# Loading the output weights in the 33rd round of scores instead of ahead of the first queries' fetches

## The chip, the cores and the metric

The kernel runs on one core of one Trainium2 chip. The metric is the time of one execution on the device, in microseconds (us). Beside it stands the span of a profiled execution, from its first to its last instruction.

## The reference

Two independent operators are computed in float32, and their outputs are put side by side. A is a long convolution whose kernel comes out of a state-space model with 576 channels and 128 states; B is attention with 32 query heads of 18 elements over 2048 positions, which all share one key and one value head.

```python
def _A_ref(u, A_re, A_im, B_re, B_im, C_re, C_im, log_dt, Dskip):
    dt = jnp.exp(log_dt)[:, None]
    logdA = dt * (A_re + 1j * A_im)
    P = jnp.exp(logdA[:, :, None] * l[None, None, :])          # l = 0..2047
    K = jnp.einsum("dn,dnl,dn->dl", Cc, P, dt * Bc).real
    ...                                                         # causal convolution of u with K
    return y + u * Dskip[None, None, :]

def _B_ref(x, wq, wk, wv, wo):
    q = (x @ wq).reshape(B, S, H, Dh).transpose(0, 2, 1, 3)     # H = 32, Dh = 18
    k, v = x @ wk, x @ wv
    p = softmax(einsum("bhqd,bkd->bhqk", q, k) * Dh ** -0.5)
    o = einsum("bhqk,bkd->bhqd", p, v)
    return o.transpose(0, 2, 1, 3).reshape(B, S, H * Dh) @ wo

return jnp.concatenate([_A_ref(...), _B_ref(...)], axis=-1)
```

The change concerns `wo`, the matrix of the last product of B.

## The kernel before, in words

**Attention.** The 2048 queries are worked in four chunks `c` of 512. In a chunk, heads are taken in pairs: a pair has its queries in one tile `aug` (two heads at partitions 0 and 64, 55 rows each: the query as a high part, again, a low part, and a row with a bound on the scores). For every block `kb` of 128 keys and every pair, `scores` (L454) makes a 128 x 1024 tile of scores with two matmuls (L461), `exponentials` (L465) turns it into P on ACT (L469), and `product` (L753) multiplies P by the values on PE (L760). A group is four heads, so two pairs; its 16 key blocks make 32 score tiles. When a group is done, its sums are copied out of PSUM (`gather`, L472, a DVE copy into `o`) and stored in DRAM (`od`). After eight groups, a chunk is normalized and multiplied by `wo` (`normalize`, `outproj`; the matmuls are at L174, in the helper `matmul4`).

**Rounds.** The main loop runs over 1024 score tiles in rounds of three (`for r in range(0, len(pairs), NS)`, L772, NS = 3), for three buffers of scores. A round issues its scores, then the products that are due and the exponentials, then fills the time left with other work (`fill`), then calls `fetch`. Round 33 is the one with r = 96; there the fourth group begins.

**Queries.** `qproj` (L325) computes the queries of some seven heads at a time. They go to DRAM (`qd`) by DMA, from POOL (L404), save those of the very first heads, which go from SP. `fetch` (L444) loads them as `aug` tiles from SP (L450) for the pairs up to five ahead, as far as they have been computed; the ring has five tiles, so a fetch also waits until PE is done with the scores of the pair that had its tile.

**The convolution** (`class Conv`) is cut into twelve pieces. Each makes tables on DVE (`tab`, L1100 and on, by the recorder at L104), kernel samples on PE (`kg`, L1124), transforms on PE (L174, with the matrix `dft`), products on DVE, and transforms back. Its transfers go by SP too.

**The order.** The order of PE, ACT and DVE is written out when the program is built: a planner with estimated costs (`Clock`, `Stream`, `fill`) decides which piece of side work goes in between the rounds. SP's loads and stores stand in the order in which the program issues them, all in one queue. `load_wo` (L320) writes five zeros with a DVE MEMSET that isn't part of the planner's estimates, then issues five loads of `wo` from SP; each waits for the MEMSET:

```python
def load_wo(self):
    self.nc.vector.memset(self.wo[0:1, :, 0:1], 0.0)
    for m, (m0, mn) in enumerate(MT):
        self.nc.sync.dma_start(self.wo[:mn, m, :], self.a["wo"][m0:m0 + mn, :])
```

In the kernel before, it is called at the head of `main` (L703). At that place the SP queue has just been given the key rows (`kaug`), the query weights, the transform matrix `dft` and the inputs `u` and `dsk` of the first two pieces of the convolution (`Conv.start`, L1277). What comes behind it is the first call of `fetch`, at the end of the first round.

Of the kernel before, what the change touches and what calls it, by code (L numbers as in the profile page):

```python
# [176 lines left out]
class Attention:  # L177
# [521 lines left out]
    def main(self, conv, flag):  # L699
        nc, K = self.nc, self.k  # L700
        conv.beside = lambda: self.o_left + self.q_left
        side = self.side_work
        self.load_wo()  # L703
        K.t = K.v = K.a = self.o_free = 0.0
        K.fill = 0.0
        side.ready = 0.0
        for st in conv.streams:
            st.ready = 0.0
        prep = Stream(self.prepare(), K, 99.0)
        pairs = [(c, g, kb, j) for c in range(NCH) for g in range(8) for kb in range(16) for j in range(2)]  # L710
        state = dict(credit=0.0, filled=0.0)

        def holder():
            return next((st for st in [side] + conv.streams if st.holds), None)

        def force(done):
            while not done():
                st = holder()
                (side if st is None else st).advance()
                self.fetch(self.group)  # L720

        def fill(then):

            t, idle = K.t, 0.0
            more = True
            while more:
                more = False
                credit = state["credit"] - (K.t - t - idle)
                urgent = self.due < self.step + 8
                late = self.late()  # L730
                for st in (prep, side, conv) if urgent else (prep, conv, side):

                    if st is side and side.kind == "p" and not (urgent or side.holds) and conv.lags(self.step):
                        continue
                    spare = credit - 0.3 if st is not side or urgent or late or side.holds else 0.0
                    wait = then - K.t - (1.2 if st is side and not urgent and not side.holds and self.units > 0.6 * self.step + HEAD else 0.15)
                    if st.go(self.step, max(spare, wait, 0.3 * (st is side and side.holds and conv.lags(self.step) and credit > -1.0)), holder()):
                        more = True
                        break
                else:  # L740

                    at = min((x for x in (st.event() for st in [prep, side] + conv.streams) if x > K.t), default=then)
                    if at < then - 0.5:
                        idle += at - K.t
                        K.t = at
                        more = True
            t += idle
            if K.t > t:
                K.t += 0.03
            state["filled"] += K.t - t  # L750
            state["credit"] = max(state["credit"] - (K.t - t), -0.8)

        def product(n):  # L753
            nonlocal o_ps
            c, g, kb, _ = pairs[2 * n]
            if kb == 0:
                fill(self.o_free)
                o_ps = self.ps_o.tile([P, CT], F32, tag="o", name=f"ops{c}_{g}")
            for j in range(4):
                nc.tensor.matmul(o_ps[32 * j:32 * j + 32, :], self.v[:, kb, :], pts[2 * n + j // 2][:, j % 2, :],  # L760
                                 start=(kb == 0), stop=(kb == 15), tile_position=(0, 32 * j))
            K.pe(0.88, done[2 * n + 1] + 0.1, self.o_free if kb == 0 else 0.0)
            read[n] = K.t + 0.2
            state["credit"] -= 0.88
            if kb == 15 and (c, g) != (NCH - 1, 7):
                self.gather(c, g, o_ps)
                if g == 7:
                    self.todo.append((c, range(5)))
                if c == NCH - 1 and g in LATE:
                    self.todo.append((c, LATE[g]))  # L770
        o_ps, pts, done, read, behind = None, {}, {}, {}, 0
        for r in range(0, len(pairs), NS):  # L772
            new = range(r, min(r + NS, len(pairs)))
            self.step = new[-1] // 2
            ss = {}
            for i in new:
                c, g, kb, j = pairs[i]
                if (g, kb, j) == (0, 0, 0):
                    self.od[c] = self.dr.tile([8 * P, CT], F32, tag="od", name=f"od{c}")
                force(lambda: 16 * c + 2 * g + j in self.ready)  # L780
                ss[i] = self.scores(i, c, 2 * g + j, kb, 0.335 if i == r else 0.215)
            K.t += 0.22
            for i in new:

                while (i - NP) // 2 >= behind:
                    product(behind)
                    behind += 1
                c, g, kb, j = pairs[i]
                pts[i] = self.exponentials(i, c, 2 * g + j, kb, *ss[i], read.get((i - NP) // 2, 0.0))
                done[i] = K.a  # L790
            s = self.step

            state["credit"] = min(state["credit"] + NS / 2 * (0.88 + min(max((TOTAL - state["filled"]) / max(LAST - s, 20), 0.45), 0.7 if s < 384 else 0.9)), 1.2 + 0.88)

            def free():

                return max(K.s[(r + NS + j) % NS] - 0.22 * j for j in range(NS))
            while behind < r // 2:
                fill(free() - 0.88 * (r // 2 - behind))

                if behind == r // 2 - 1 and K.t + 0.88 > free() + DEFER:
                    break
                product(behind)
                behind += 1
            fill(free())
            c, g, kb, j = pairs[new[-1]]
            self.group = (new[-1] + 1) // 32
            self.fetch(self.group)
            nxt = 16 * c + 2 * g + 3
            if kb >= 12 and nxt < 64:  # L810
                force(lambda: nxt in self.ready)
        while behind < len(pairs) // 2:
            product(behind)
            behind += 1

        while self.todo or self.busy or holder() or any(m == 0 for _, _, m in self.rest):
            if self.todo or self.busy:
                prep.advance()
            elif holder() or self.outs:
                (holder() or side).advance()  # L820
        conv.drain()
        nc.vector.tensor_scalar(flag, self.ubound[0:1, :], LIMIT / (2 * SCALE), None, op0=ALU.is_le)
        self.finish(NCH - 1, self.part, o_ps, self.w4, self.b4)
# [596 lines left out]
```

## Time and profile before

| | |
|---|---|
| runs shown | 1220.51, 1227.37, 1228.71 us; median 1227.37 |
| the profiled execution's own time | 1227.15 us |
| its span | 1224.8 us |
| mean granted PE clock | 0.985 of full speed |
| PE busy | 1146.8 us (94%) |
| ACT busy | 1032.8 us (84%) |
| DVE busy | 983.7 us (80%) |
| moved by DMA | 102.13 MB |

PE is TensorE (matmuls; PEld are its weight loads), ACT ScalarE, DVE VectorE, POOL GpSimd, SP SyncE; a q behind the name (SPq) means the engine's queue, which issues DMAs. A row of a timeline gives the start in us, the duration in us, engine, line, operation and tiles (out<-in), shape and count; the bracket at its end is the time the engine was idle just before, and what ended it ("issue": nothing that the profile shows). A row of waits gives the total in us, the number of times and the longest. A row of stretches gives the stretch, its length, the busy time of PE, PEld, DVE, ACT and POOL with their counts, then the granted PE clock, the busy share of the DMA engines and the GB/s moved. Rows of DMA queues give packets, MB and the share of 16 engines.

### The profile page before, as it was taken

To read this page: it belongs to the slowest core of one execution; us is meant where nothing else is said; L and a number is where in the kernel's file an instruction comes from. 1 tells how busy PE (TensorE), PEld (TensorE's weight loads), DVE (VectorE), ACT (ScalarE), POOL (GpSimd) and SP (SyncE) were. 2 spreads that over 40 slices of the span, in tenths; PEclk is the share of its full clock that TensorE was granted. 3 is DMA by queue.
4 is the path that set the end of the run, shared out by engine and by line. 5 is a ranking of instruction groups with operands and counts; after the bars stand their busy time and mean duration, and the time that the engine had idled before them with its cause. 6 is when DMAs were issued, how large, how long until landed. Compare 5 with 4: busy or idle time off the path is not lost.

```text
span 1224.8 us, 32944 instructions
## 1 busy us (share of the span) xinstructions
PE 1146.8 (94%) x13852; PEld 469.6 (38%) x13852; DVE 983.7 (80%) x1608; ACT 1032.8 (84%) x1091; POOL 119.2 (10%) x210
## 2 busy tenths in 40 slices
PE   5989899999899999899999989999989999899997
PEld 1434333444243434334344324444333444334333
DVE  4758988987988976895897996897998896796653
ACT  2778889889889888988888988888889888998993
POOL 2230310120310000011020000001150000000000
PEclk9999899999899999999999999999989999999999
DMA  7542323123343112213224011313142313012111
GB/s 225 149 139 81 127 79 101 51 64 96 107 131 107 35 38 93 81 39 113 82 90 145 28 71 54 102 52 105 37 123 88 106 36 90 21 51 82 35 40 42
DMA packets 61712, 102.13 MB, mean 83 GB/s; under 512 B 17692, under 2 KB 28570, under 8 KB 61048
## 3 DMA queue, kind: packets, MB, share of 16 engines
q1 hardware_dynamic: 47046, 85.32, 21.7%
q0 software_dynamic: 13824, 14.07, 4.5%
q8 instruction: 110, 1.80, 0.6%
q10 hardware_dynamic: 690, 0.60, 0.2%
q14 instruction: 42, 0.34, 0.1%
HBM read 55.66 MB, written 42.89 MB: 80 GB/s over the span
## 4 chain that ended last, share of the span: by engine, by line
PE 64%; DVE 21%; ACT 6%; DMA 4%; issue 4%; POOL 0%; SPq 0%; DVEq 0%; ACTq 0%
PE ops L760 26%; PE s L461 19%; ACT P L469 6%; PE op L174 5%; DVE tab L104 3%; PE q L339 3%; DVE acc L104 3%; DVE ks L104 3%; PE kg L1124 3%; PE iy L174 3%; DVE pt L104 2%; DMA xr<-xT 2%; PE hu L174 1%; PE hk L174 1%; DVE o L108 1%
## 5 line engine op out<-in xcount | busy, mean ns | idle before, releaser
L469 ACT ACTIVATE P<-s 128x1024 f32<-128x1024 f32 x1024 | 967.9, 1030 | 156.4 <-PE s L461 154.3
L760 PE MATMUL ops<-P,v_sb 128*32 128x512 f32 x4096 | 520.3, 604 | 8.2 <-DVE o L108 8.0
L461 PE MATMUL s<-aug,kaug 55*128 55x512 f32 x2048 | 362.1, 441 | 23.7 <-ACT P L469 19.0
L461 PEld LDWEIGHTS s<-aug,kaug 55*128 55x128 f32 x2048 | 168.9, 185 | 328.9 <-ACT P L469 281.4
L760 PEld LDWEIGHTS ops<-P,v_sb 128*32 128x32 f32 x4096 | 115.3, 110 | 161.2 <-issue 123.1
L404 POOL DMA_DIRECT2D qd<-qh x116 | 67.2, 585 | 536.0 <-DVE qh L108 535.9
L174 PE MATMUL op<-wo_sb,oT 126*32 126x288 f32 (+1 forms) x1112 | 83.1, 423 | 7.3 <-DVE ob L108 5.5
L339 PE MATMUL q<-x,wq_sb 128*32 128x256 f32 x1360 | 87.5, 391 | 1.0 <-DVE un L116 1.0
L108 DVE COPY ksb<-kg 128x192 f32<-128x192 f32 x48 | 17.4, 362 | 62.9 <-PE kg L1124 61.7
L104 DVE TENSOR_TENSOR tab<-tab 128x576 f32<-128x576 f32 (+1 forms) x72 | 59.1, 821 | 1.5
L104 DVE TENSOR_TENSOR tab<-tab,tt 128x576 f32<-128x576 f32 (+1 forms) x72 | 59.1, 820 | 1.5
L339 PEld LDWEIGHTS q<-x,wq_sb 128*32 128x32 f32 x1360 | 41.2, 112 | 47.9 <-issue 22.3
L104 DVE TENSOR_TENSOR tt<-f,sum 128x576 f32<-128x576 f32 (+1 forms) x72 | 58.8, 816 | 0.0
L104 DVE TENSOR_TENSOR tab<-sum,r 128x576 f32<-128x576 f32 (+1 forms) x72 | 58.7, 816 | 0.0
L104 DVE TENSOR_TENSOR tab<-r,dif 128x576 f32<-128x576 f32 (+1 forms) x72 | 58.7, 815 | 0.0
L174 PEld LDWEIGHTS op<-wo_sb,oT 126*32 126x32 f32 (+1 forms) x1112 | 32.9, 112 | 53.5 <-issue 21.8
L104 DVE TENSOR_TENSOR acc<-acc,pt 128x1728 f32<-128x1728 f32 (+2 forms) x36 | 48.7, 1353 | 0.5
L104 DVE TENSOR_TENSOR pt<-us,ks 128x1728 f32<-128x1728 f32 (+2 forms) x36 | 48.6, 1350 | 0.2
L1124 PEld LDWEIGHTS kg<-tab 128*32 128x32 f32 x2304 | 36.0, 110 | 24.5 <-issue 10.8
L1124 PE MATMUL kg<-tab 128*32 128x64 f32 x2304 | 41.7, 220 | 2.1 <-DVE tab L104 1.3
L104 DVE TENSOR_TENSOR ks<-ks 128x576 f32<-128x576 f32 (+1 forms) x48 | 40.9, 852 | 0.7
L104 DVE TENSOR_TENSOR u<-u,iy 128x384 f32<-128x384 f32 x24 | 13.3, 554 | 31.7 <-PE iy L174 31.4
(134 smaller groups left out, 967.1 us busy)
## 6 DMA issues: line engine op xcount, KB each, us to landing
aug<-qd SPq DMA_DIRECT2D x124, 110.0 KB
od<-o SPq DMA_DIRECT2D x31, 256.0 KB
fr<-stage SPq DMA_DIRECT2D x10, 624.0 KB
qd<-qh POOLq DMA_DIRECT2D x24, 216.0 KB, 4.3
u<-u SPq DMA_DIRECT2D x12, 384.0 KB
kd<-ksb SPq DMA_DIRECT2D x12, 384.0 KB
kt<-kd SPq DMA_DIRECT2D x48, 96.0 KB
outa<-u SPq DMA_DIRECT2D x12, 384.0 KB
```

The source lines that it names most:

```text
L104: return self.v.tensor_tensor(out, *a, **k)
L108: return self.v.tensor_copy(out, *a, **k)
L174: nc.tensor.matmul(ps[j:e], w[:, j:e], x, start=start, stop=stop, tile_position=(0, j))
L339: nc.tensor.matmul(ps[o, 256 * f:256 * f + 256], w[:, k, i], xt[:, k, x], start=(k == 0), stop=(k == 4), tile_position=(0, 32 * j))
L404: q.dma_start(qd[h:h + n, row + d:row + d + nd, cs], src[i1:i1 + n * nd, :cs.stop - cs.start].bitcast(F32))
L461: nc.tensor.matmul(ps[:, j, :], self.kaug[r, kb * P:(kb + 1) * P], t[r, :], start=True, stop=True)
L469: nc.scalar.activation(pt, ps, AF.Exp, scale=SCALE)
L760: nc.tensor.matmul(o_ps[32 * j:32 * j + 32, :], self.v[:, kb, :], pts[2 * n + j // 2][:, j % 2, :], start=(kb == 0), stop=(kb == 15), tile ...
L1124: nc.tensor.matmul(ps[32 * g:32 * g + 32, d, :], t[:, :32], t[:, 32:], start=(j == 0), stop=(j == 1), tile_position=(0, 32 * g))
```

## The change

The call of `load_wo` is taken out of the head of `main` and put into round 33, behind that round's scores, products and exponentials and ahead of its fill. `load_wo` itself, its MEMSET and its five loads are the same. Nothing else changes, and the planner's estimates are the same with and without it.

```diff
--- before.py
+++ after.py
@@ -700,7 +700,6 @@
         nc, K = self.nc, self.k
         conv.beside = lambda: self.o_left + self.q_left
         side = self.side_work
-        self.load_wo()
         K.t = K.v = K.a = self.o_free = 0.0
         K.fill = 0.0
         side.ready = 0.0
@@ -789,6 +788,9 @@
                 pts[i] = self.exponentials(i, c, 2 * g + j, kb, *ss[i], read.get((i - NP) // 2, 0.0))
                 done[i] = K.a
             s = self.step
+            if r == 96:
+
+                self.load_wo()
 
             state["credit"] = min(state["credit"] + NS / 2 * (0.88 + min(max((TOTAL - state["filled"]) / max(LAST - s, 20), 0.45), 0.7 if s < 384 else 0.9)), 1.2 + 0.88)
```

## The prediction

> **What bounds the kernel now.** I read the page first, for what the whole span is made of; then the waits of PE in time order, because PE carries the chain; then the order of the SP queue around the five loads that move; then the same at the place they move to.
>
> ```profile
> span 1224.8 us, 32944 instructions
> PE 1146.8 (94%) x13852; PEld 469.6 (38%) x13852; DVE 983.7 (80%) x1608; ACT 1032.8 (84%) x1091; POOL 119.2 (10%) x210
> PE 64%; DVE 21%; ACT 6%; DMA 4%; issue 4%; POOL 0%; SPq 0%; DVEq 0%; ACTq 0%
> q8 instruction: 110, 1.80, 0.6%
> ```
>
> PE is busy for 94% of the span and carries 64% of the chain that ended last; transfers carry only 4% of it. A moved load is therefore worth something only where PE stands still because of it. The order of instructions on PE, ACT and DVE is written out by the planner and does not change, so what PE loses in one place it does not make up by doing something else first. The last row is needed below: 110 transfers of instructions of 16 KB each, beside 2 x 13852 PE instructions, make one such transfer for about 252 PE instructions. That is PE's own code, which arrives while it runs.
>
> The only long stop of PE near the moved loads is in the first 80 us. The timeline of PE and of ACT there:
>
> ```profile
> 58.59 1.90 PE L760 MATMUL ops<-P,v_sb 128*32 128x512 f32 x16
> 66.29 0.28 PE L174 MATMUL up<-sel_sb,aw 128*32 128x8 f32 x16
> 68.92 0.73 PE L461 MATMUL s<-aug,kaug 55*128 55x512 f32 x4 [2.35 <-issue]
> 70.01 0.46 PE L461 MATMUL s<-aug,kaug 55*128 55x512 f32 x1 [0.35 <-DMA aug<-qd]
> 70.65 0.61 PE L461 MATMUL s<-aug,kaug 55*128 55x512 f32 x1 [0.18 <-DMA aug<-qd]
> 71.19 3.44 PE L760 MATMUL ops<-P,v_sb 128*32 128x512 f32 x16
> 74.56 0.96 PE L461 MATMUL s<-aug,kaug 55*128 55x512 f32 x6
> ...
> 64.44 2.86 ACT L469 ACTIVATE P<-s 128x1024 f32<-128x1024 f32 x3 [0.19 <-PE s L461]
> 69.55 2.86 ACT L469 ACTIVATE P<-s 128x1024 f32<-128x1024 f32 x3 [2.25 <-PE s L461]
> 75.19 5.61 ACT L469 ACTIVATE P<-s 128x1024 f32<-128x1024 f32 x6 [2.78 <-PE s L461]
> ```
>
> Three things are to be seen. At 66.57 PE stops for 2.35 us with nothing named that it waits for. Then the two score matmuls of the next pair of heads wait 0.35 and 0.18 us for their queries (aug). Then sixteen products take 3.44 us where sixteen of the same took 1.90 us at 58.59. ACT pays for all of it: 2.25 and 2.78 us idle, against 0.19 in the round before.
>
> ```profile
> 58.00:62.00 4.00, 4.00 (x80) 1.85 (x82) 2.26 (x4) 3.30 (x4) 2.17 (x4) 1.00 0.96 228
> 62.00:66.00 4.00, 4.00 (x94) 1.71 (x82) 0.69 (x3) 3.81 (x5) 2.36 (x5) 1.00 0.99 289
> 66.00:70.00 4.00, 1.31 (x28) 0.64 (x21) 3.90 (x12) 1.75 (x3) 0.50 (x1) 1.00 0.86 295
> 70.00:74.00 4.00, 3.82 (x18) 0.94 (x18) 3.55 (x5) 2.40 (x3) 0.61 (x1) 0.61 0.64 226
> ...
> q1 hardware_dynamic: 1133, 2.27, 90.8%
> q0 software_dynamic: 148, 0.12, 5.0%
> q14 instruction: 2, 0.02, 0.4%
> ...
> q8 instruction: 1, 0.02, 4.0%
> ```
>
> The first four rows are four stretches (last three columns: granted clock, busy share of the DMA engines, GB/s). The transfers are saturated from 58 to 70 (0.96, 0.99, 0.86) and the clock is 0.61 right after the stop. The rows behind the first "..." are the queues of the nine microseconds from 57 to 66: no instruction transfer of q8 at all. The last is from 66 to 68: there it is. In the eight microseconds from 58 to 66 PE issued 80 + 82 + 94 + 82 = 338 instructions, more than the 252 of one transfer. So I read the unnamed 2.35 us as PE having run out of code, its next block standing behind other transfers.
>
> What stood there, from the timeline of the SP queue, its waits from 52 to 75, and the sizes:
>
> ```profile
> 54.66 0.60 SPq L964 DMA_DIRECT2D u<-u  x1
> 55.86 4.39 SPq L323 DMA_DIRECT2D wo_sb<-wo  x5
> 61.13 9.84 SPq L450 DMA_DIRECT2D aug<-qd  x10
> ...
> SPq L450 <- DMA wo_sb<-wo: 4.1, 4, 2.0
> SPq L450 <- DMA u<-u: 1.6, 1, 1.6
> ...
> wo_sb<-wo SPq DMA_DIRECT2D x4, 283.5 KB
> wo_sb<-wo SPq DMA_DIRECT2D x1, 162.0 KB
> ```
>
> The five wo loads are issued from 55.86 to 60.25, the first query fetches only from 61.13, and these wait another 4.1 us in all for wo loads to land before SP may issue on. The wo loads are 4 x 283.5 + 162 = 1296 KB, 1.33 MB, which at the 289 GB/s of 62 to 66 is 4.6 us of all the transfer capacity there is.
>
> **The change part by part.**
>
> (1) The five loads leave the front of the queue. The queries that PE used at 70.01 and 70.65 lay behind 4.6 us of wo; without it they are there by about 65.4 to 66.0, and the round that needs them could begin its third score at about 67.3 (the exponential that frees the last score buffer ends at 64.44 + 2.86). The 0.53 us of named waiting goes, with over a microsecond to spare. The code block appears after 66.0; to cost nothing it must come 2.35 us earlier, and 4.6 us of transfers ahead of it are gone. So that wait goes too, by about the same spare. Without the stop the slow products, 3.44 against 1.90, lose their cause: 1.54 us. By PE: 2.35 + 0.35 + 0.18 + 1.54 = 4.42. By ACT: 2.25 + 2.78 less two ordinary gaps of 0.19 = 4.65. I take 4.5. Bounds: at most the whole idle time of ACT, 5.03; at least the named waits alone, 0.53, if the code comes no earlier. Below nothing is excluded here, since nothing is put in the place that is left.
>
> The Trainium skill (page "Runtime: NRT & Kernel Launch", section "Instruction fetch mechanics") speaks against my reading: it has code come in blocks of 256 instructions, the next while the present one runs, and calls the cost mostly hidden. The block size agrees with the 252 of the page row; "hidden" does not agree with an unnamed stop of 2.35 us that ends after the missing block came. By that rule the stop has another cause and stays, and the sum would be 0.53 us.
>
> (2) Does DVE let the gain through? It must have been idle here, since PE's products feed it:
>
> ```profile
> 79.69 0.69 DVE L108 COPY o<-ops 128x512 f32<-128x512 f32 x1 [6.07 <-PE ops L760]
> ```
>
> It stood 6.07 us waiting for this very product. A shift of 4.5 to 5.0 fits into that with 1 us left, and what DVE does next starts from this copy. If that cover were gone, the gain would be cut to what DVE has idle. So the later work on all engines moves forward as one block.
>
> (3) The loads arrive in the 33rd round. The order of SP there, what DVE does, and the stretches:
>
> ```profile
> 153.69 1.59 SPq L450 DMA_DIRECT2D aug<-qd  x4
> 162.09 0.34 SPq L478 DMA_DIRECT2D od<-o  x1
> ...
> 158.57 0.69 DVE L108 CAST qh<-q 128x512 fp32r<-128x512 f32 x1 [1.27 <-PE q L339]
> ...
> 152.00:156.00 4.00, 4.00 (x50) 1.50 (x42) 3.83 (x8) 3.67 (x5) 0.00 (x0) 1.00 0.30 103
> 156.00:160.00 4.00, 4.00 (x40) 1.64 (x36) 2.69 (x4) 3.35 (x5) 0.45 (x1) 1.00 0.16 49
> 160.00:164.00 4.00, 3.13 (x26) 0.80 (x22) 3.96 (x10) 3.03 (x4) 4.00 (x8) 1.00 0.48 128
> ...
> L321 DVE MEMSET wo_sb<- x1: 62/62/62, 31.7 to 31.7; 1x5 f32 x1
> L174 PE MATMUL op<-wo_sb,oT x1112: 402/406/690, 411.6 to 1203.8; 126*32 126x288 f32 x154, 72*32 72x288 f32 x32
> ```
>
> The four fetches at 153.69 end the 32nd round's work, so the loads stand behind them, wait for their MEMSET (62 ns) in DVE's order, and stand ahead of the store of o at 162.09. SP has nothing to issue from 155.28 to 162.09, 6.8 us; five issues took 4.39 us with their waits at the old place. So SP is late for nobody. The MEMSET goes ahead of a 1.27 us idle of DVE: nothing, and 0.06 us if that idle were gone. The 1.33 MB fall on DMA engines busy 0.16 to 0.48; they are through in some 5 to 7 us. Nobody waits for them before 411.6. What is behind them on SP (the store of o, later loads for the convolution) and on POOL (the queries of later heads, of which the first are used many rounds on) is not in demand there. PE's code: 50 + 42 + 40 + 36 + 26 + 22 = 216 instructions in 12 us, so one block lasts about 14 us here against 6 us at the front; a block that comes 5 us late is still in time. I put this part at nothing, bounded below by nothing and above by the price of the third rival.
>
> **Sum.** The profiled execution took 1227.15 us, 2.35 around its span of 1224.8. 1227.15 - 4.5 + 0.0 = 1222.65, which I give as 1222.6. The three runs shown have the median 1227.37, so this execution stands for them; but they spread from 1220.51 to 1228.71.
>
> **Rivals.** *First: the code comes no earlier.* u, the fetches themselves and POOL's stores of queries still fill the engines from 58 to 66, and the block may stand behind all of these just as well. Against it: 1.33 MB of what passed before it is gone. Gain 0.53, time 1226.6. The same time comes out of the skill's rule above. Chance 0.17.
>
> *Second: the gain is taken back.* PE reaches a later wait sooner and stands there longer, because DVE is at its own pace. For it: DVE is 21% of the chain. Against it: its 6.07 us of idle and its start from PE's product. With all taken back 1227.1; chance 0.10.
>
> *Third, the other side: the wo loads starve PE's code at the new place.* If the next block is asked for just as the loads begin and PE has less than about 5 us of instructions left, PE stops for the whole 4.6 us of the burst, some 1.3 us for the block (4.0% of 16 engines over the two microseconds from 66 to 68), and 1.54 us of slow products: 7.4, less 4.5 gained in front: +2.9, time 1230. It decides from the point where fewer than some 100 instructions (5 us at 216 in 12 us) are left. Against it: a block lasts 14 us there. Chance 0.05.
>
> *Fourth: the change does not do what it says*, the loads still being issued ahead of the fetches. Against it: SP's rows stand in the order of the program. 1227.1, chance 0.02.
>
> **How the numbers follow.** The forecast has 0.66, with its own range 1221 to 1225.5 (5.03 gained, or a part of the code wait left). The range over the cases reaches up past the first and second rival, to 1228, and down to 1218: the best sum, 1222.1, less half of the 8.2 us over which the three runs spread. It leaves out the third rival. No case comes near 1%, about 12 us, which is what a measurement of this kernel can tell from no change: within it 0.93, and 0.04 faster and 0.03 slower are for mechanisms that I don't see.
>
> **What would show it.** Right: no unnamed wait of PE near 67 and no wait of scores for aug; ACT gaps under 0.5 us between 64 and 72; clock 1.00 from 70 to 74; the aug fetches issued from about 56 to 57; the wo loads issued between about 150 and 158, with PE and ACT no idler there; the product copy o now at about 75. Wrong in the first step: an unnamed wait of 1 us or more still at 66 to 69. Wrong in the second: the copy at 75, and yet the same time at 200. Wrong in the third: a new unnamed wait of PE within 15 us of the wo issues.

## The result, and the profile after

| | before | after |
|---|---|---|
| median of 16 runs each, us | 1225.28 (1220.37 to 1228.71) | 1219.03 (1214.76 to 1221.75) |
| ratio after to before | | 0.995, interval 0.9934 to 0.9965 |
| profiled execution, us | 1227.15 | 1219.4 |
| its span, us | 1224.8 | 1217.6 |

The kernel is 4.3 to 8.1 us shorter (the interval times 1225.28); 4.5 were forecast. That lies within 1% of no change. The median of 1219.03 lies in the range over the cases, 1218 to 1228, and below the forecast's own range, 1221 to 1225.5; the point on the time, below, says why. I go through the profile in the order of the prediction. The page of the kernel after, three rows:

```profile
span 1217.6 us, 32944 instructions
PE 1138.1 (93%) x13852; PEld 467.4 (38%) x13852; DVE 983.4 (81%) x1608; ACT 1032.9 (85%) x1091; POOL 119.3 (10%) x210
PE 63%; DVE 23%; ACT 6%; issue 4%; DMA 3%; POOL 1%; SPq 1%; DVEq 0%; ACTq 0%
```

The work is the same to the instruction. PE's busy time is 8.7 us less, 1146.8 against 1138.1; a PE at half clock counts as busy for longer. The stretch in which it had stopped, from the timelines of PE and of ACT after:

```profile
65.57 0.28 PE L174 MATMUL up<-sel_sb,aw 128*32 128x8 f32 x16
65.78 1.34 PE L461 MATMUL s<-aug,kaug 55*128 55x512 f32 x6
67.05 1.92 PE L759 MATMUL ops<-P,v_sb 128*32 128x512 f32 x16
68.91 0.97 PE L461 MATMUL s<-aug,kaug 55*128 55x512 f32 x6
...
63.72 5.61 ACT L469 ACTIVATE P<-s 128x1024 f32<-128x1024 f32 x6 [0.19 <-PE s L461]
69.54 5.61 ACT L469 ACTIVATE P<-s 128x1024 f32<-128x1024 f32 x6 [0.21 <-PE s L461]
```

The scores follow `up` at once: no unnamed wait, no wait for aug, and the sixteen products take 1.92 us in place of 3.44. ACT goes through six exponentials without a gap. The stretches there and at the new place, then the queue of instruction transfers between 61.0 and 62.7, DVE's copy of that product, and SP's queue:

```profile
66.00:70.00 4.00, 3.89 (x32) 1.32 (x34) 3.86 (x8) 3.79 (x5) 0.61 (x1) 1.00 0.47 140
70.00:74.00 4.00, 3.97 (x54) 1.71 (x50) 2.86 (x4) 4.00 (x5) 0.00 (x0) 1.00 0.00 1
150.00:154.00 4.00, 4.00 (x40) 1.64 (x36) 3.11 (x6) 3.34 (x5) 0.56 (x2) 1.00 0.69 225
154.00:158.00 4.00, 3.13 (x28) 0.91 (x30) 3.96 (x10) 3.03 (x4) 4.00 (x7) 1.00 0.84 242
...
q8 instruction: 1, 0.02, 4.4%
...
74.03 0.69 DVE L108 COPY o<-ops 128x512 f32<-128x512 f32 x1 [1.14 <-PE ops L759]
...
54.81 13.03 SPq L450 DMA_DIRECT2D aug<-qd  x10
147.56 1.59 SPq L450 DMA_DIRECT2D aug<-qd  x4
150.19 2.04 SPq L323 DMA_DIRECT2D wo_sb<-wo  x5
155.98 0.35 SPq L478 DMA_DIRECT2D od<-o  x1
```

The clock is 1.00 where it was 0.61. The code block that came after 66 us is now on its way before 62.7. DVE's wait for the product is 1.14 us of the 6.07 there were. The weights are issued from 150.19, in the gap of SP that was forecast, and the DMA engines carry them there at 0.69 and 0.84 with PE no idler (4.00 and 3.13, against 4.00 and 3.13 in the same work of before, at 156 to 164).

### The profile page after: what moved, and what is told of

Its sections match the earlier page's. It is cut to its first block, busy times and chain, and to the rows that moved or that the text cites. A ratio compares the mean times of both kernels' runs of the same rounds, so it can differ in the third digit from the quotient of the medians.

```text
span 1217.6 us, 32944 instructions
## 1 busy us (share of the span) xinstructions
PE 1138.1 (93%) x13852; PEld 467.4 (38%) x13852; DVE 983.4 (81%) x1608; ACT 1032.9 (85%) x1091; POOL 119.3 (10%) x210
## 4 chain that ended last, share of the span: by engine, by line
PE 63%; DVE 23%; ACT 6%; issue 4%; DMA 3%; POOL 1%; SPq 1%; DVEq 0%; ACTq 0%
PE ops L759 26%; PE s L461 19%; ACT P L469 6%; PE op L174 5%; DVE acc L104 3%; DVE ks L104 3%; PE q L339 3%; DVE tab L104 3%; PE kg L1126 3%; PE iy L174 3%; DVE pt L104 2%; DMA xr<-xT 2%; PE hu L174 1%; PE hk L174 1%; DVE o L108 1%
## 5 line engine op out<-in xcount | busy, mean ns | idle before, releaser
L108 DVE COPY ksb<-kg 128x192 f32<-128x192 f32 x48 | 17.4, 363 | 62.7 <-PE kg L1126 62.6
```

Source lines behind the costliest of these rows:

```text
L108: return self.v.tensor_copy(out, *a, **k)
```

## The experiments

**Theory:** PE takes its instructions in blocks of 256; at 66 us its next block lay behind the weights and the queries; with 1.33 MB out of the way it comes in time. **Rivals:** the stop was something of the new pair's queries or of ACT; or it belongs to the weights as such, and not to what stands ahead of the block; or any place but the first is as good.

The runs are told apart by the r of the loop, three to a round: r = 96 is the 33rd round, r = 201 the 68th; where an expectation says "round 201", it means that r. Three ways of reading serve all runs. *The gain at the place* is how much earlier than in the kernel before the 34th exponential starts, less the same for the 28th. In the kernel before these start at 75.19 and 64.44, 10.75 us apart; after, at 69.54 and 63.72, 5.82 apart: 4.93 us gained. It doesn't contain what differs elsewhere between two executions. *PE's instructions are numbered* from 0 in the order of their starts in the trace (27,878 to 27,881 records in a trace, with weight loads and the like). *The instruction transfers* of 16 KB are numbered in the order in which they begin. In the quiet start of the kernel the first two begin just as PE issues its instructions 170 and 426, that is 256n - 86, and I take that as the moment at which block n is asked for. It is good to about 1 us only: in the fourteen traces some transfers begin ahead of it, by 0.9 us at the most (block 45).

| run | median us | ratio to before, interval | gain at the place |
|---|---|---|---|
| after, again | 1220.04 | 0.9959, 0.9940 to 0.9978 | 4.92 |
| weights behind the first queries | 1221.29 | 0.9964, 0.9947 to 0.9981 | 4.12 |
| three of five loads in front | 1219.33 | 0.9947, 0.9929 to 0.9966 | 3.99 |
| `u` moved instead of the weights | 1221.11 | 0.9971, 0.9955 to 0.9987 | 4.92 |
| `u` moved too | 1219.70 | 0.9954, 0.9938 to 0.9971 | 4.93 |
| ten small stores, r = 111 | 1221.17 | 0.9951, 0.9933 to 0.9970 | 4.94 |
| three large stores, r = 609 | 1221.58 | 0.9970, 0.9954 to 0.9986 | 4.93 |
| the same, r = 600 | 1221.04 | 0.9970, 0.9953 to 0.9987 | 4.93 |
| five large stores, r = 609 | 1219.38 | 0.9955, 0.9939 to 0.9971 | 4.94 |
| the same, r = 594 | 1220.18 | 0.9955, 0.9936 to 0.9973 | 4.93 |
| weights at r = 201 | 1221.69 | 0.9959, 0.9942 to 0.9975 | 4.92 |
| weights at r = 198 | 1219.46 | 0.9946, 0.9931 to 0.9961 | 4.92 |

The ratios do not tell these twelve from one another, since a loss of 1 us is below their intervals; the places in the trace do.

**After, again** (no edit).

> The changed kernel once more, to be compared on the same chip with the others. Every theory: about 6 us under the kernel before (ratio 0.995), no unnamed wait of PE near 67 us.

No stop, and the same gain at the place. 4.92 / 1225.3 would make a ratio of 0.9960, and 0.9959 was measured, 0.9940 to 0.9978: the gain at the place accounts for it as far as the medians can tell, and the 0.995 of the first comparison is the same within its interval.

**The weights behind the first queries, still in front of the code.**

```diff
-            if r == 96:
+            if r == 15:
                 self.load_wo()
```

> The wo loads are called in the 6th round (r = 15), so in SP's queue they stand behind the first six query fetches, and the same 1.33 MB still pass in the first 75 us. Theory (PE's next code block stands behind what was queued ahead of it, and only that): SP holds the loads back until older transfers have landed, at about 60 to 63, so the block asked for at about 61 is ahead of most of them; an unnamed wait of PE near 66 of 0 to 0.7 us, no wait for aug, time 4 to 6 us under the kernel before. Rival (saturated transfer engines starve PE's code as long as they are saturated, whatever the order): an unnamed wait of 2 us or more as before, no wait for aug, time 0.5 to 1.5 us under the kernel before. Rival (the late queries were the whole of it): the full gain, no unnamed wait.

SP, PE and ACT of this kernel:

```profile
54.77 5.28 SPq L450 DMA_DIRECT2D aug<-qd  x6
61.71 2.56 SPq L323 DMA_DIRECT2D wo_sb<-wo  x5
...
67.97 0.28 PE L174 MATMUL up<-sel_sb,aw 128*32 128x8 f32 x16
69.37 0.97 PE L461 MATMUL s<-aug,kaug 55*128 55x512 f32 x6 [1.12 <-ACT P L469]
...
66.12 2.85 ACT L469 ACTIVATE P<-s 128x1024 f32<-128x1024 f32 x3 [0.18 <-PE s L461]
70.00 5.61 ACT L469 ACTIVATE P<-s 128x1024 f32<-128x1024 f32 x6 [1.03 <-PE s L461]
```

The queries are there and nothing waits for them, and yet PE stands still for 1.12 us at the same instruction. The profile names ACT. But ACT itself stands idle for 1.03 us waiting for just these scores. In the kernel after the scores start at 65.78 with the same three exponentials (63.72 and on) still running. So the name is only the last semaphore that came, with the end of the third exponential at 68.97 (66.12 + 2.85), and PE goes on 0.40 us later; in the kernel before that end was at 67.30, 1.62 us before PE went on at 68.92, and the profile names nothing. It is the same stop. The queries are not its cause. At 1.12 us it lies between what the theory gave (0 to 0.7) and what the rival of saturated transfers gave (2 or more), so neither holds as it stood. At the place it costs 4.93 - 4.12 = 0.81 us.

**Three loads in front, two in the 33rd round.**

```diff
-    def load_wo(self):
-        self.nc.vector.memset(self.wo[0:1, :, 0:1], 0.0)
-        for m, (m0, mn) in enumerate(MT):
+    def load_wo(self, ms):
+        self.nc.vector.memset(self.wo[0:1, ms[0]:ms[-1] + 1, 0:1], 0.0)
+        for m in ms:
+            m0, mn = MT[m]
...
+        self.load_wo((0, 1, 2))
         K.t = K.v = K.a = self.o_free = 0.0
...
-                self.load_wo()
+                self.load_wo((3, 4))
```

> Three of the five loads (0.87 MB) stay in front, two (0.46 MB, 1.6 us at 289 GB/s) move to the 33rd round. Theory: the code block comes about 1.6 us earlier than in the kernel before, so the unnamed wait of PE shrinks from 2.35 to 0.5 to 1.0 us, named waits for aug go, and the gain is 2.5 to 4.5 us of the whole 5 to 6. Rival (an all-or-nothing matter): the wait stays at 2.35 or is gone.

SP, PE and ACT:

```profile
54.84 1.62 SPq L324 DMA_DIRECT2D wo_sb<-wo  x3
57.21 13.08 SPq L451 DMA_DIRECT2D aug<-qd  x10
...
68.24 0.96 PE L462 MATMUL s<-aug,kaug 55*128 55x512 f32 x6 [1.25 <-ACT P L470]
...
68.86 5.61 ACT L470 ACTIVATE P<-s 128x1024 f32<-128x1024 f32 x6 [1.16 <-PE s L462]
```

The stop is 1.25 us, over the 0.5 to 1.0 expected: with 850 of 1296 KB in front, about half of the 2.35 us stays. It costs 0.94 us at the place (4.93 - 3.99). No product runs at half clock behind it, here or behind the 1.12 us of the run above.

**Another load out of the way, the weights left in front.** `u` of the second piece of the convolution (384 KB) and its `dsk` (96 KB) are taken out of `Conv.start` and called in the 33rd round, and the weights stay where they were before.

```diff
+        self.load_wo()
         K.t = K.v = K.a = self.o_free = 0.0
...
             if r == 96:
-
-                self.load_wo()
+                conv.load_u(1)
...
         self.load_u(0)
-        self.load_u(1)
```

> The kernel before, wo loaded in front as there, but the second piece's inputs (u, 393 KB, moved to the 33rd round; its dsk, 98 KB, comes about where it can) are taken out of the queue ahead of it: 0.4 to 0.5 MB, 1.4 to 1.7 us, fewer ahead of the queries and of the code block. Theory (bytes ahead of the block count, whatever they belong to): about as the run with three wo loads in front, an idle time of PE of 0.5 to 1.5 us near 67, no or a short wait for aug, no slow products, gain 3 to 6.5 us. Rival (something of the wo loads themselves): the stop of 2.35 us and the wait for aug stay, gain under 1 us.

```profile
54.51 2.42 SPq L323 DMA_DIRECT2D wo_sb<-wo  x5
58.45 6.35 SPq L450 DMA_DIRECT2D aug<-qd  x6
...
67.30 1.35 PE L461 MATMUL s<-aug,kaug 55*128 55x512 f32 x6
```

SP's and PE's rows: all five weights are in front, and the stop is gone, with the whole gain of 4.92. So the weights have nothing to do with it as such: another load out of the way does as well. It did better than expected, though. A stop of 0.5 to 1.5 us was forecast, as with three loads in front, and none came. There 446 KB (0.46 MB) were out of the way, here 480 KB (0.49 MB), nearly the same, and yet the block began 4.04 us after it was asked for there and 1.79 us here. So the sum of bytes taken out does not set the delay; what else does, the runs do not show.

**Both moved.** The kernel after, with the two lines of `load_u(1)` moved as above.

> The changed kernel with the second piece's inputs moved to the 33rd round as well. Theory: the block has about 3 us to spare in the changed kernel already, so nothing more is gained: time as the changed kernel within 1 us. Rival (every byte taken out of the front is worth time): 1 to 2 us less.

No stop and the same gain at the place (`dsk` went at 59.11 already, behind six fetches). There is nothing more to be had there. The block began 2.40 us after it was asked for, against 0.83 in the kernel after, with less in front of it.

**Can transfers stop PE elsewhere?** In the next five runs the loaded weights are also stored into scratch arrays that nobody reads; the kernel computes the rest as before. A one-row copy on DVE holds the stores back to their round.

```diff
+    def burst(self):
+        self.nc.vector.tensor_copy(self.wo[0:1, :, 0:1], self.wo[0:1, :, 0:1])
+        for n in range(3):
+            t = self.dr.tile([P, 4, D], F32, tag=f"t{n}", name=f"t{n}")
+            self.nc.sync.dma_start(t[:126], self.wo[:126, 0:4, :])
...
+            if r == 609:
+                self.burst()
```

First ten small stores (2,304 bytes a row, one per piece of `wo` and twice over) at r = 111:

> The changed kernel, and in round r = 111 ten stores of the wo tile from SBUF into scratch in DRAM that nobody reads (2.65 MB), issued from about 168 us. No query and nothing else that PE needs stands behind them; PE asks for a code block at about 171 and uses its last instruction in hand at about 177 in the changed kernel, because two bursts of 48 small matmuls come in between. Theory: the block arrives only behind the burst, PE stops with no named reason near 177 for 1 to 4 us, and runs slow products after it if the stop is long; time 1.5 to 6 us above the changed kernel. Rival (the stop at 67 came from the queries): no unnamed wait near 177, time as the changed kernel within 1 us.

Then the three of the diff at r = 609, and, as a control, at r = 600, where the block has longer:

> The changed kernel, and in round r = 609 three stores of the wo tile from SBUF into scratch in DRAM that nobody reads (3 x 1.16 MB in rows of 9 KB), issued from about 736 to 738 us. At about 743 PE asks for a block, in a stretch with two bursts of 48 small matmuls, so the block before is used up in 5.0 us (748). No query and nothing else that PE needs soon stands behind the stores. Theory: the block arrives behind the stores, about 4 to 8 us after it was asked for; PE stops from about 748 until 1.3 us after the block has arrived (in the kernel before and in the runs with the loads behind the queries and with three in front, PE went on 1.32 us after the end of the block's transfer each time): an idle time of 1 to 5 us that no wait for queries explains, slow products after it if it is over 2 us; time 1 to 6 us above the changed kernel. Rival (the stop at 67 came from the queries or the score buffers): no stop, time as the changed kernel within 1 us.

> The same three stores in round r = 600, from about 724 to 726 us. The block that is asked for in that stretch (at about 732) has 11 us until the one before is used up. Theory: no stop of PE between 724 and 744, time as the changed kernel within 1 us. Rival (3.5 MB of extra transfers cost PE time wherever they are): a stop here too, time as in the run with the burst on the short block.

Then five instead of three, 5.8 MB, at r = 609, and as a control at r = 594:

> The changed kernel with five extra stores of the loaded output weights to a scratch array (5.8 MB in all, nothing reads it), from about 735 us. The store of three such pieces kept TensorE's next block of instructions waiting until they had drained, 4.1 us, and it landed just when it was needed. Theory (the block stands behind whatever is queued for the DMA engines): the drain moves from 746.5 to about 752, the block asked for at about 742.5 lands at about 753 and is needed at about 747.5. TensorE stops with no operand missing at about 748.3, for 4 to 6 us, goes on about 1.3 us after the landing, its next products run at half clock, and the median lies 1 to 6 us over that of the changed kernel. Rival (the stop at 67 us was something of the queries' rows or of the scores' first use, not code): no operand of TensorE moves here, so no unnamed wait near 748, and a time within 1.5 us of the changed kernel's.

> The same five stores some 15 rounds earlier, from about 719 us, so that they drain at about 737. Theory: the block asked for at about 732 is late by 4 to 6 us but is needed only at about 744, so no stop, and the time is within 1.5 us of the changed kernel's. Rival (the bytes themselves or the slowed transfers cost the time): the same loss as with the stores at the later place.

PE did not stop in any of the five. At r = 111 and 609 that was against what my theory had expected, and so were the times; at r = 600 and 594 it was expected. At r = 111 the block asked for at 174.44 began 3.26 us later, but PE had 8.01 us until it needed it. PE with five large stores, and the queues between 742.3 and 746.6:

```profile
746.41 1.90 PE L765 MATMUL ops<-P,v_sb 128*32 128x512 f32 x16
748.24 0.97 PE L467 MATMUL s<-aug,kaug 55*128 55x512 f32 x6
749.14 1.07 PE L765 MATMUL ops<-P,v_sb 128*32 128x512 f32 x8
...
734.67 2.15 PE L174 MATMUL op<-wo_sb,oT 126*32 126x288 f32 x32 [0.62 <-DVE wo_sb L326]
...
q1 hardware_dynamic: 209, 1.62, 97.0%
```

The block asked for at 742.31 was held up by 4.39 us, hardly more than the 4.14 behind three stores, while the stores kept the DMA engines busy until about 755: the next block, asked for at 747.28, came only at 754.89, when the burst had nearly drained, and found 5.72 us to spare. So a block does not always stand behind all that is queued, as I had expected; the first one passed after a share. Here 209 packets on 16 engines, 13 each, went first; ahead of the next block it was 337, 21 each, and in the kernel before 718 packets of queue 1 in the rows below, 45 each. The Trainium skill ("DMA: Bandwidth & Descriptors", section "Queues, rings and completion order") says that each engine takes turns between its queues, draining one bundle of some 9 to 17 descriptors, at most 64, before it turns to the next. If a packet of the profile is such a descriptor, 13 lies in the usual range and 21 and 45 below the ceiling; the rings themselves, and which engine carried the block, no trace here shows, so an engine with a shorter queue of its own would look the same. The only loss that the burst causes PE between 728 and 765 us is the wait for the copy that gates it, the 0.62 us in the fourth row.

**The weights at a bad place.** No extra transfers: `load_wo` alone at r = 201, or at r = 198.

```diff
-            if r == 96:
+            if r == 201:
                 self.load_wo()
```

> The changed kernel with the output weights loaded in round 201 in place of 96: five pieces issued from about 263.6 to 265.6 us. A block of TensorE's instructions is asked for at about 263.2, is served at 265.1 in the changed kernel and is needed at 268.3. Theory: it now stands behind the weights, is served at about 268, lands at 269, and TensorE stops at about 268.7 for 1 to 2.5 us with no operand named; the time is 0 to 3 us over the changed kernel's. Rival (the place does not matter as long as the weights are not in front of queries): no stop near 268, the changed kernel's time.

> The same load in round 198, issued from about 262.1 to 264.1 us, before or as the block is asked for. Theory: served at 266.5 to 267.5, landed at 267.5 to 268.5, so a stop of 0 to 1.2 us near 268.7 and a time within 1.5 us of the changed kernel's. Rival (the place does not matter): no stop at all.

At r = 201, SP's row, PE's and ACT's:

```profile
263.89 2.08 SPq L323 DMA_DIRECT2D wo_sb<-wo  x5
...
268.34 0.83 PE L1126 MATMUL kg<-tab 128*32 128x64 f32 x42
269.82 0.31 PE L1126 MATMUL kg<-tab 128*32 128x64 f32 x6 [0.65 <-issue]
...
270.67 2.85 ACT L469 ACTIVATE P<-s 128x1024 f32<-128x1024 f32 x3 [1.32 <-PE s L461]
```

This is the run that settles it. PE stops for 0.65 us inside a run of 48 products of one line and one operand, after the 42nd: all 48 have the same `tab` to wait for, so it can't be an operand. It is shorter than the 1 us that I expected at least, since the block passed after 210 packets (263.6 to 266.7), 3.20 us late and not 5. The next row is the queue of instructions between 266.7 and 268.2 in this run:

```profile
q8 instruction: 1, 0.02, 5.3%
```

That is the missing block; PE goes on behind it. ACT's gap of 1.32 us is 0.38 in the kernel after:

```profile
269.34 2.85 ACT L469 ACTIVATE P<-s 128x1024 f32<-128x1024 f32 x3 [0.38 <-PE s L461]
```

So the stop costs 0.94 us at its place, too little for the medians to show. One round earlier, at r = 198:

```profile
261.10 2.04 SPq L323 DMA_DIRECT2D wo_sb<-wo  x5
...
268.61 0.85 PE L1126 MATMUL kg<-tab 128*32 128x64 f32 x48
```

There the same 48 products run through; the block began at 265.71, ahead of the 266.5 to 267.5 expected. The place does matter, and by less than 3 us.

**The blocks of all these runs together.** Numbered as above, PE goes on after its stop with instruction 1217 in the three kernels that stop in front, and with 6081 at r = 201. These are 4 x 256 + 193 and 23 x 256 + 193: four stops on four programs, at scores and in the middle of `kg`, all on the same step of 256. So block n is needed at instruction 256n + 193:

| kernel | block | asked for | begins | landed | needed instruction runs | from landing to it | PE |
|---|---|---|---|---|---|---|---|
| before | 4 | 61.33 | 66.31 | 67.60 | 68.92 | 1.32 | stops 2.35 |
| weights behind queries | 4 | 63.01 | 66.94 | 68.05 | 69.37 | 1.32 | stops 1.12 |
| three in front | 4 | 61.74 | 65.78 | 66.92 | 68.24 | 1.32 | stops 1.25 |
| weights at r = 201 | 23 | 263.63 | 266.83 | 268.11 | 269.82 | 1.71 | stops 0.65 |
| five stores, r = 609 | 66 | 742.31 | 746.70 | 747.63 | 749.15 | 1.52 | runs on |
| `u` moved instead | 4 | 62.13 | 63.92 | 65.07 | 67.23 | 2.16 | runs on |
| weights at r = 198 | 23 | 263.89 | 265.71 | 266.74 | 269.17 | 2.43 | runs on |
| after | 4 | 60.61 | 61.44 | 62.64 | 65.71 | 3.07 | runs on |
| five stores, r = 594 | 65 | 730.64 | 735.96 | 736.89 | 742.21 | 5.32 | runs on |

In all fourteen traces, with 108 blocks each, the needed instruction never runs less than 1.32 us after its block has landed. The limit is not sharper than some 0.4 us: the stop at r = 201 ended 1.71 us after the landing, while block 55 passes without a stop at 1.45 to 1.62 us in thirteen of the traces. The same five stores that came 0.2 us short of a stop at r = 609 (1.52 against 1.32) were 4 us away from one at r = 594 (5.32). For the kernel before, the queues while block 4 waited (61.3 to 66.2):

```profile
q1 hardware_dynamic: 718, 1.33, 87.9%
q0 software_dynamic: 166, 0.13, 10.0%
q14 instruction: 2, 0.02, 1.1%
```

## Why the prediction was right, point by point

**What bounds it: code.** Right, and shown: the stop falls on a step of 256 instructions, moves with the landing of the block, goes when other bytes are moved, and appears at another place inside one run of products. The rule that code loading is mostly hidden (the Trainium skill, "Runtime: NRT & Kernel Launch", section "Instruction fetch mechanics"), which the prediction weighed with a sum of 0.53 us, holds for 1508 of the 1512 blocks of PE in the fourteen traces, behind which PE does not stop, and fails for four, one in each of four kernels. Its 256 instructions per block are confirmed.

**Step 1, 4.5 us.** Every term was there: 2.35, 0.35, 0.18 and 1.54 us are gone. That the last belongs to the stop rests on the one profile of the kernel before; more on that at the end of this section. The block landed 4.96 us earlier (62.64 against 67.60), where the 4.6 us of the weights were counted on. The size was a little low: 4.93. By ACT I had taken off two ordinary gaps of 0.19 us from 5.03. Only one is left, 0.21 ahead of 69.54; and six exponentials in one go take 5.61 us where two threes take 2 x 2.86, 0.11 less. 5.03 - 0.21 + 0.11 = 4.93. The fetches left at 54.81, somewhat ahead of the 56 to 57 forecast.

**Step 2, the gain gets through.** Right. The copy came at 74.03, about 75 forecast; the lead over the kernel before is 5.65 us at the 34th exponential and 6.11 at the 91st, and the same 6.1 still at the 241st. The 0.72 us of it that were there ahead of the stop are not the change's, see below; nor are, it seems, the 0.45 us that come between the 90th and the 91st (139.0 to 144.2 us), where both kernels run at half clock (granted clock 0.51 from 136 to 143 after, 0.57 from 142 to 150 before).

**Step 3, the new place costs nothing.** Right: the lead is 6.11 us at the 91st exponential (144 us) and at the 151st (206 us), on either side of the loads. What was said there of a block that lasts 14 us is now more exact: a block is asked for some 279 instructions before it is needed (86 + 193), and at the new place these take 15.8 us (block 12, asked for at 145.20) and 13.9 (block 13, at 159.22). In front they took 5.2 (61.33 to the end of `up` at 66.57), at r = 201 5.3. But the margin was not put to the test there: no block was asked for while the weights went, from 151 to 158. Block 13 began 3.69 us after it was asked for, while POOL's stores of queries ran, and landed with 9.29 us to spare.

**The time.** 1222.65 was formed from an execution at 1227.15. The median of 16 runs of before is 1225.28, so 1.9 us of the 3.6 us between forecast and measured median are that execution, 0.4 are step 1, and the remaining 1.3 lie within the interval. Had the sum started from 1225.28, the forecast's own range would have reached down to 1219.1. The two spans differ by 7.2 us, 2.3 more than the 4.93. This is where PE's half-clock spells fall, in two stretches of before and then the same two of after:

```profile
34.00:37.00 3.00, 3.00 (x38) 1.32 (x30) 2.93 (x5) 1.86 (x3) 0.00 (x0) 0.54 0.19 46
900.00:904.00 4.00, 4.00 (x37) 1.21 (x26) 3.93 (x6) 2.08 (x3) 3.09 (x6) 0.57 0.71 193
...
34.00:37.00 3.00, 3.00 (x50) 1.58 (x46) 2.93 (x6) 2.65 (x4) 0.00 (x0) 1.00 0.20 50
900.00:904.00 4.00, 2.88 (x22) 0.74 (x14) 2.01 (x5) 4.00 (x5) 1.64 (x3) 1.00 0.28 77
```

They are not the change's: the kernel after has such a spell in its second profile where it had none in the first (52 to 56 us, first the second profile, then the first):

```profile
52.00:56.00 4.00, 4.00 (x35) 1.47 (x32) 1.31 (x2) 1.94 (x2) 0.00 (x0) 0.57 0.54 166
...
52.00:56.00 4.00, 4.00 (x50) 1.49 (x42) 0.44 (x1) 2.99 (x4) 0.00 (x0) 1.00 0.82 273
```

**The rivals.** The first and the second fell with the trace after. The third, the weights starving the code at their new place, is a real mechanism that was priced too high: at r = 201 it stops PE for 0.65 us and costs 0.94, not 7.4, since there the block passed after 3.20 us and not after all that was queued. The fourth fell, but its argument was wrong: SP's rows do not all stand in the order in which the program issues them, as the text ahead of the prediction has it too. With `load_u(1)` moved to the 33rd round, its `dsk`, which the program issues behind `u`, left at 65.73 and `u` at 151.74:

```profile
65.73 0.36 SPq L967 DMA_DIRECT2D dsk<-dsk  x1
...
151.74 0.36 SPq L966 DMA_DIRECT2D u<-u  x1
```

**Half clock behind the stop of 2.35 us, and not behind those of 1.12 and 1.25.** No run varied that alone, but the traces show a pattern. In each of the fourteen, all changes of the granted clock lie on one grid of 3.41 us, which begins elsewhere from one execution to the next. I take the slots of that grid at full clock and ask for PE's busy share in each. All 48 with less than 0.41 are followed by half clock, none of the 4549 with 0.72 or more, and 41 of the 201 in between. These are the slots with the stops: of the kernel before, of the weights behind the first queries, and of three loads in front.

```profile
67.47:70.88 3.41, 1.43 (x6) 0.66 (x6) 3.28 (x7) 1.33 (x2) 0.23 (x1) 1.00 0.79 295
...
68.39:71.80 3.41, 2.43 (x22) 0.90 (x22) 3.29 (x8) 2.38 (x3) 0.61 (x1) 1.00 0.73 241
...
65.71:69.12 3.41, 2.16 (x54) 1.08 (x42) 2.92 (x11) 2.25 (x4) 0.50 (x1) 1.00 0.80 277
```

PE's share is 1.43 / 3.41 = 0.42 in the first, 0.71 and 0.63 in the others. From 0.41 to 0.45 half clock followed in 20 of 24 slots, from 0.60 to 0.72 in 6 of 85. So the longer stop, with the waits for aug behind it, left PE idle for most of one slot. Had the grid of that execution lain otherwise, the stop would have been split over two slots; whether the 1.54 us come in every execution of the kernel before is therefore open. It also fits that some spells recur in all traces (one begins between 135 and 143 us, one between 321 and 331; PE stands still there for 5.05 and 4.81 us in the kernel after) and others do not. In the twelve runs above no such spell begins between 57 and 130 us.

## What to carry to other kernels

An unnamed wait ("issue"), or one for a releaser that had long been done, in a stretch of many short PE instructions under busy DMA engines is worth a count: number PE's instructions, and see whether the stop falls on a step of 256 and ends some 1.3 us after an instruction transfer has landed. If so, move a large load out of the few microseconds in which 279 instructions run quickly. It need not be the one that stands right ahead: here 0.49 MB of another load did as well as the 1.33 MB of the weights, while 0.46 MB of the weights left a stop of 1.25 us. A place where the 279 instructions took 11.6 us bore 5.8 MB of transfers without a stop. The gain is read at the place, between two marks on either side, since the medians of single variants differ by less than their intervals.

## What the runs showed of the hardware that I had not expected

- In the four stops a block of PE's code began 3.2 to 5.0 us after it was asked for; the longest delays of the traces are 7.6 us (the second block behind five large stores) and 7.4 (block 81, in the same run, long after the stores), with time to spare. The delay of the first block behind the stores hardly grew with the queue (4.14 us behind three, 4.39 behind five).
- Between the landing of a block and the first instruction out of it lie 1.32 us at least (three stops to the hundredth, the fourth 1.71).
- All changes of PE's granted clock in a trace lie on one grid of 3.41 us, and every slot of it at full clock in which PE was busy for less than 0.41 was followed by half clock (48 of 48); from 0.72 on none was (of 4549).
- The profile gives such a stop two different names, "issue" or the engine whose semaphore came last (ACT), for the very same instruction: "issue" where that semaphore came 1.62 us before PE went on, ACT where it came 0.40 us before.
